# A fused causal convolution and RWKV channel mix: from batch-by-batch chunks to stacked batch pairs and a fixed program order

## The chip, the cores and the metric

One core of a Trainium2 chip runs the whole program. The metric is the device time of one execution in microseconds (us). The core has five engines that run side by side and wait for each other through semaphores: TensorE (PE in the profile; PEld is its weight load), VectorE (DVE), ScalarE (ACT), GpSimd (POOL) and SyncE (SP), whose queue issues DMAs. Each works through its own queue in order.

## The reference

x has 8 batches of 4160 tokens with 192 channels, float32. A causal convolution with 7 taps comes first; its weights are the softmax of an 8 x 7 table, one row for each head of 24 channels. The result goes through a channel mix:

```python
# softmax over the 7 taps, then for every batch, token s, head h
y[s, h] = sum_k w[h, k] * y_in[s + k - 6, h]      # zeros before the first token
x_prev = y shifted down by one token, first row zero
xk = mu_k * y + (1 - mu_k) * x_prev
xr = mu_r * y + (1 - mu_r) * x_prev
k  = maximum(xk @ w_k, 0)          # 192 -> 1024
v  = (k * k) @ w_v                 # 1024 -> 192
r  = sigmoid(xr @ w_r)             # 192 -> 192
out = r * v                        # float32
```

## The kernel before

Batches are processed one after the other, each in 33 blocks of 128 tokens and 9 chunks of 512 tokens (the last of 64). The kernel is written with a planner that orders the instructions of each engine itself; the program's text only gives dependencies and priorities.

Setup (lines 52 to 160): softmax of the taps; its 56 numbers go to DRAM and back so that every partition has them (`w_scr`, `wbc`). From 13 shifted masks, VectorE builds for each head two 128 x 128 banded matrices, `lm` for the block itself (L112, L116) and `lc` for the corner that reaches into the block before (L126, L130). Weights are loaded and cast to bf16 by ScalarE.

For each batch:

- `emit_xload`: for each block of 128 tokens, one DMA of 96 KB brings x (`x_f`, three buffers), and GpSimd casts it to bf16 and sorts it by head (`xb`, L177). The next batch's loads are spread over the chunks of the batch at hand.
- Convolution: for each head two matmuls over up to 21 blocks at once add up in `psum_c` (L196, L203); ScalarE (L211) and VectorE (L216) take turns in copying the result to `y_all`.
- `emit_tr`: each block is transposed in two halves of 96 channels (L225), and copied to `yT` by VectorE (L234) or ScalarE (L238). Channels now lie on partitions, 96 of the 128, twice.
- `emit_mix`: GpSimd forms `diff_t`, the difference of neighbouring tokens (L255); VectorE makes xk and xr from it, two instructions each (L262, L270).
- `emit_kstage`: for each of 8 tiles of d_ff two matmuls of 512 columns into `psum_k` (L289), a relu by ScalarE to `k_sb` (L298), and for each pair of tiles a square by VectorE to `k2_all` (L302; the profile calls it `k_all`).
- `emit_rv`: for each 128 tokens two matmuls for r (L322) and a sigmoid (L329), eight matmuls for v (L338), for each pair a product on VectorE (L349), and one output DMA for each 128 tokens.

In PSUM, `psC` and `psA` (for k) have two buffers each, as have `psB_tr` and `psB_vr`; r and v share the last.

Of the kernel before, what the change touches and what calls it, by code (L numbers as in the profile page):

```python
# [7 lines left out]
FP32 = mybir.dt.float32  # L9
# [6 lines left out]
def kernel(  # L16
# [18 lines left out]
    HC = D // 2  # L35

    NBLK = (S + P - 1) // P
    LAST_ROWS = S - (NBLK - 1) * P
    NB_GRP = 21
    CHUNK = 512  # L40
    NF = DF // P

    const = ctx.enter_context(tc.tile_pool(name="const", bufs=1))
    wpool = ctx.enter_context(tc.tile_pool(name="wts", bufs=1))
    perb = ctx.enter_context(tc.tile_pool(name="perb", bufs=2))
    small = ctx.enter_context(tc.tile_pool(name="small", bufs=3))
    stream = ctx.enter_context(tc.tile_pool(name="stream", bufs=3))
    psA = ctx.enter_context(tc.tile_pool(name="psA", bufs=2, space=bass.MemoryType.PSUM))
    psB = ctx.enter_context(tc.tile_pool(name="psB", bufs=2, space=bass.MemoryType.PSUM))
    dram = ctx.enter_context(tc.tile_pool(name="dram", bufs=1, space=bass.MemoryType.DRAM))  # L50

    w_raw = const.tile([H, K], FP32)
    nc.sync.dma_start(out=w_raw, in_=weight)
# [10 lines left out]
    w_soft = const.tile([H, K], FP32)  # L64
    nc.vector.tensor_scalar(
        out=w_soft, in0=w_exp, scalar1=w_rcp, scalar2=None, op0=ALU.mult
    )
    w_scr = dram.tile([H, K], FP32)
    nc.sync.dma_start(out=w_scr, in_=w_soft)
    wbc = const.tile([P, H, K], FP32)  # L70
    wbc_src = bass.AP(
        tensor=w_scr.tensor,
        offset=w_scr.offset,
        ap=[[0, P], w_scr.ap[-2], w_scr.ap[-1]],
    )
    nc.sync.dma_start(out=wbc, in_=wbc_src)

    ones_t = const.tile([P, P], BF16)
    nc.vector.memset(ones_t, 1.0)
    mmask = []  # L80
    for dlt in range(K):
        m = const.tile([P, P], BF16, tag=f"mmask{dlt}")
        nc.gpsimd.affine_select(
            out=m,
            in_=ones_t,
            pattern=[[1, P]],
            compare_op=ALU.is_equal,
            fill=0.0,
            base=-dlt,
            channel_multiplier=-1,  # L90
        )
        mmask.append(m)
    cmask = {}
    for dlt in range(1, K):
        m = const.tile([P, P], BF16, tag=f"cmask{dlt}")
        nc.gpsimd.affine_select(
            out=m,
            in_=ones_t,
            pattern=[[1, P]],
            compare_op=ALU.is_equal,  # L100
            fill=0.0,
            base=P - dlt,
            channel_multiplier=-1,
        )
        cmask[dlt] = m
    ident = mmask[0]

    Lmain = []
    Lcorner = []
    for h in range(H):  # L110
        lm = const.tile([P, P], BF16, tag=f"lm{h}")
        nc.vector.tensor_scalar(  # L112
            out=lm, in0=mmask[0], scalar1=wbc[:, h, K - 1 : K], scalar2=None, op0=ALU.mult
        )
        for dlt in range(1, K):
            nc.vector.scalar_tensor_tensor(  # L116
                out=lm,
                in0=mmask[dlt],
                scalar=wbc[:, h, K - 1 - dlt : K - dlt],
                in1=lm,  # L120
                op0=ALU.mult,
                op1=ALU.add,
            )
        Lmain.append(lm)
        lc = const.tile([P, P], BF16, tag=f"lc{h}")
        nc.vector.tensor_scalar(  # L126
            out=lc, in0=cmask[1], scalar1=wbc[:, h, K - 2 : K - 1], scalar2=None, op0=ALU.mult
        )
# [12 lines left out]
    wk_sb = wpool.tile([HC, 2, DF], BF16)
    for cc in range(2):
        nc.sync.dma_start(out=wk_f32[:, cc, :], in_=moe_w_k[cc * HC : (cc + 1) * HC, :])
    nc.scalar.copy(out=wk_sb, in_=wk_f32)
    wr_f32 = wpool.tile([HC, 2, D], FP32, tag="wr_f32")
    wr_sb = wpool.tile([HC, 2, D], BF16)
    for cc in range(2):
        nc.sync.dma_start(out=wr_f32[:, cc, :], in_=moe_w_r[cc * HC : (cc + 1) * HC, :])
    nc.scalar.copy(out=wr_sb, in_=wr_f32)
    wv_f32 = wpool.tile([P, NF, D], FP32, tag="wv_f32")  # L150
    wv_sb = wpool.tile([P, NF, D], BF16)
    for f in range(NF):
        nc.sync.dma_start(out=wv_f32[:, f, :], in_=moe_w_v[f * P : (f + 1) * P, :])
    nc.scalar.copy(out=wv_sb, in_=wv_f32)
    mu_f32 = wpool.tile([HC, 2, 2], FP32, tag="mu_f32")
    for cc in range(2):
        nc.sync.dma_start(out=mu_f32[:, 0, cc : cc + 1], in_=moe_mu_k[cc * HC : (cc + 1) * HC])
        nc.sync.dma_start(out=mu_f32[:, 1, cc : cc + 1], in_=moe_mu_r[cc * HC : (cc + 1) * HC])
    mu_bf = wpool.tile([HC, 2, 2], BF16, tag="mu_bf")
    nc.scalar.copy(out=mu_bf, in_=mu_f32)  # L160


    x_bufs = {}

    def emit_xload(bb, jlist):
        if bb not in x_bufs:
            xb = perb.tile([P, H, NBLK + 1, G], BF16, tag="x_bf")
            nc.vector.memset(xb[:, :, 0, :], 0.0)
            x_bufs[bb] = xb
        xb = x_bufs[bb]  # L170
        for j in jlist:
            rows = P if j < NBLK - 1 else LAST_ROWS
            x_f32 = stream.tile([P, D], FP32, tag="x_f32")
            nc.sync.dma_start(
                out=x_f32[:rows, :], in_=x[bb, j * P : j * P + rows, :]
            )
            nc.gpsimd.tensor_copy(  # L177
                out=xb[:rows, :, j + 1, :],
                in_=x_f32[:rows, :].rearrange("p (h g) -> p h g", h=H),
            )  # L180
            if rows < P:
                nc.vector.memset(xb[rows:, :, j + 1, :], 0.0)

    emit_xload(0, range(NBLK))

    for b in range(B):
        x_bf = x_bufs.pop(b)
        yT = perb.tile([HC, 2, 1 + NBLK * P], BF16, tag="yT")
        nc.vector.memset(yT[:, :, 0:1], 0.0)

        y_all = perb.tile([P, NBLK, H, G], BF16, tag="y_all")
        for g0 in range(0, NBLK, NB_GRP):
            nb = min(NB_GRP, NBLK - g0)
            for h in range(H):
                psum_c = psA.tile([P, NB_GRP * G], FP32, tag="psC")
                nc.tensor.matmul(  # L196
                    out=psum_c[:, : nb * G],
                    lhsT=Lmain[h],
                    rhs=x_bf[:, h, g0 + 1 : g0 + 1 + nb, :],
                    start=True,  # L200
                    stop=False,
                )
                nc.tensor.matmul(  # L203
                    out=psum_c[:, : nb * G],
                    lhsT=Lcorner[h],
                    rhs=x_bf[:, h, g0 : g0 + nb, :],
                    start=False,
                    stop=True,
                )
                if h % 2 == 0:  # L210
                    nc.scalar.copy(  # L211
                        out=y_all[:, g0 : g0 + nb, h, :],
                        in_=psum_c[:, : nb * G].rearrange("p (n g) -> p n g", g=G),
                    )
                else:
                    nc.vector.tensor_copy(  # L216
                        out=y_all[:, g0 : g0 + nb, h, :],
                        in_=psum_c[:, : nb * G].rearrange("p (n g) -> p n g", g=G),
                    )

        def emit_tr(jjlist, dve_evac):
            for jj in jjlist:
                psum_tr = psB.tile([P, 2, P], BF16, tag="psB_tr")
                for cc in range(2):
                    nc.tensor.transpose(  # L225
                        out=psum_tr[:HC, cc, :],
                        in_=y_all[:, jj, :, :].rearrange("p h g -> p (h g)")[
                            :, cc * HC : (cc + 1) * HC
                        ],
                        identity=ident,  # L230
                    )
                t0 = jj * P
                if dve_evac:
                    nc.vector.tensor_copy(  # L234
                        out=yT[:, :, 1 + t0 : 1 + t0 + P], in_=psum_tr[:HC, :, :]
                    )
                else:
                    nc.scalar.copy(  # L238
                        out=yT[:, :, 1 + t0 : 1 + t0 + P], in_=psum_tr[:HC, :, :]
                    )  # L240
# [176 lines left out]
```

## Time and profile before

| | |
|---|---|
| three runs | 726.43, 729.37, 730.36 us; median 729.37 |
| span of the profiled execution | 723.8 us; its own whole time is not listed beside it |
| busy: TensorE, VectorE, ScalarE, GpSimd | 605.2, 592.5, 405.3, 296.2 us |
| TensorE matmuls / VectorE instructions | 4576 / 1109 |
| mean granted TensorE clock | 0.960 |
| DMA | 53.72 MB, mean 74 GB/s |

A group row of the profile reads: line, engine, operation, output<-inputs, shapes, count | busy us, mean ns of one | idle time of the engine just before these instructions and what ended it. A timeline row reads: start us, duration us, engine, line, operation, count of the merged instructions, and in brackets the idle time ahead and what ended it. Matmuls overlap in TensorE's pipe, so the mean duration of one is longer than the time that it adds.

### The profile page before, as it was taken

To read this page: it belongs to the slowest core of one execution; us is meant where nothing else is said; L and a number is where in the kernel's file an instruction comes from. 1 tells how busy PE (TensorE), PEld (TensorE's weight loads), DVE (VectorE), ACT (ScalarE), POOL (GpSimd) and SP (SyncE) were. 2 spreads that over 40 slices of the span, in tenths; PEclk is the share of its full clock that TensorE was granted. 3 is DMA by queue.
4 is the path that set the end of the run, shared out by engine and by line. 5 is a ranking of instruction groups with operands and counts; after the bars stand their busy time and mean duration, and the time that the engine had idled before them with its cause. 6 is when DMAs were issued, how large, how long until landed. Compare 5 with 4: busy or idle time off the path is not lost.

```text
span 723.8 us, 13091 instructions
## 1 busy us (share of the span) xinstructions
PE 605.2 (84%) x4576; PEld 396.8 (55%) x4576; DVE 592.5 (82%) x1109; ACT 405.3 (56%) x975; POOL 296.2 (41%) x353
## 2 busy tenths in 40 slices
PE   0268889798898898988898888988898988989977
PEld 0034557555574565645575555745566565645655
DVE  5969997698967999599977789689985889768994
ACT  3027556474566555655565654565565655746554
POOL 3546674476206751176305752067312123022330
PEclk9999989999999999999999998999999899978999
DMA  5413435234112321234112331124111011200112
GB/s 140 121 47 93 119 105 148 72 104 118 37 58 81 102 85 51 64 88 127 50 56 69 110 102 45 56 80 116 58 55 48 1 47 43 67 25 23 45 45 68
DMA packets 77297, 53.72 MB, mean 74 GB/s; under 512 B 9264, under 2 KB 77040, under 8 KB 77232
## 3 DMA queue, kind: packets, MB, share of 16 engines
q1 hardware_dynamic: 77232, 52.90, 24.8%
q8 instruction: 35, 0.57, 0.4%
q14 instruction: 30, 0.25, 0.1%
HBM read 27.31 MB, written 25.56 MB: 73 GB/s over the span
## 4 chain that ended last, share of the span: by engine, by line
PE 52%; DVE 34%; POOL 6%; issue 4%; ACT 3%; DMA 2%; DVEq 0%; POOLq 0%; SPq 0%; ACTq 0%
PE psum_k L289 22%; PE psum_v L338 17%; DVE k_all L302 10%; DVE xk_t L262 7%; DVE xr_t L270 6%; PE psum_r L322 5%; POOL diff_t L255 5%; DVE o_sb L349 4%; PE psum_tr L225 2%; PE psum_c L196 2%; DVE lm L116 2%; PE psum_c L203 2%; DVE yT L234 2%; DVE lc L130 2%; ACT k_sb L298 1%
## 5 line engine op out<-in xcount | busy, mean ns | idle before, releaser
L298 ACT ACTIVATE k_sb<-psum_k 128x512 bf16<-128x512 f32 (+1 forms) x576 | 298.0, 560 | 215.4 <-PE psum_k L289 173.6
L289 PE MATMUL psum_k<-xk_t,wk_sb 96*128 96x512 bf16 (+1 forms) x1152 | 316.2, 377 | 21.4 <-DVE xk_t L262 17.7
L255 POOL TENSOR_TENSOR diff_t<-yT 96x1024 bf16<-96x1024 bf16 (+1 forms) x72 | 143.6, 2000 | 322.2 <-ACT yT L238 173.2
L302 DVE TENSOR_TENSOR k_all<-k_sb 128x1024 bf16<-128x1024 bf16 (+1 forms) x288 | 206.5, 739 | 39.0 <-ACT k_sb L298 38.2
L338 PE MATMUL psum_v<-wv_sb,k_all 128*128 128x192 bf16 (+1 forms) x2112 | 197.5, 247 | 2.0 <-ACT r_all L329 1.8
L338 PEld LDWEIGHTS <-k_all 128*128 128x128 bf16 (+1 forms) x2112 | 178.4, 99 | 25.3 <-issue 5.1
L177 POOL CAST xb<-x_f 128x192 bf16<-128x192 f32 (+1 forms) x264 | 151.1, 588 | 79.2 <-DMA x_f<-in_x_dram 77.7
L289 PEld LDWEIGHTS <-wk_sb 96*128 96x128 bf16 x1152 | 108.8, 101 | 113.0 <-issue 68.5
L262 DVE SCALAR_TENSOR_TENSOR xk_t<-diff_t,mu_bf,yT 96x512 bf16<-96x512 bf16 x144 | 120.5, 839 | 32.1 <-POOL diff_t L255 32.1
L270 DVE SCALAR_TENSOR_TENSOR xr_t<-diff_t,mu_bf,yT 96x512 bf16<-96x512 bf16 x144 | 120.9, 841 | 0.0
L322 PE MATMUL psum_r<-wr_sb,xr_t 96*128 96x192 bf16 x528 | 89.6, 258 | 32.1 <-DVE o_sb L349 23.5
L329 ACT ACTIVATE r_all<-psum_r 128x192 bf16<-128x192 f32 (+1 forms) x264 | 83.3, 338 | 37.8 <-PE psum_r L322 37.5
L322 PEld LDWEIGHTS <-xr_t 96*128 96x128 bf16 x528 | 49.6, 102 | 79.5 <-issue 38.5
L349 DVE TENSOR_TENSOR o_sb<-psum_v,r_all 128x384 f32<-128x384 f32 x128 | 68.7, 548 | 23.3 <-PE psum_v L338 23.1
L225 PE MATMUL psum_tr<-m,y_all 128*96 128x128 bf16 x528 | 68.7, 227 | 21.8 <-DVE yT L234 19.6
L225 PEld LDWEIGHTS <-y_all 128*96 128x96 bf16 x528 | 57.6, 128 | 50.8 <-issue 26.3
L196 PE MATMUL psum_c<-xb,lm 128*128 128x288 bf16 (+1 forms) x128 | 45.0, 356 | 38.0 <-POOL xb L177 30.2
L211 ACT CAST y_all<-psum_c 128x504 bf16<-128x504 f32 (+1 forms) x64 | 31.5, 492 | 50.7 <-PE psum_c L203 49.5
L234 DVE COPY yT<-psum_tr 96x256 bf16<-96x256 bf16 x200 | 49.9, 278 | 3.6 <-PE psum_tr L225 3.1
L216 DVE CAST y_all<-psum_c 128x504 bf16<-128x504 f32 (+1 forms) x64 | 36.1, 565 | 17.4 <-PE psum_c L203 17.3
L203 PE MATMUL psum_c<-xb,lc 128*128 128x288 bf16 (+1 forms) x128 | 45.3, 358 | 0.0
L203 PEld LDWEIGHTS <-lc 128*128 128x128 bf16 x128 | 13.1, 102 | 31.7 <-issue 28.4
(28 smaller groups left out, 88.0 us busy)
## 6 DMA issues: line engine op xcount, KB each, us to landing
x_f<-in_x_dram SPq DMA_DIRECT2D x256, 96.0 KB, 1.9
out_dram<-o_sb SPq DMA_DIRECT2D x256, 96.0 KB, 1.7
wk_f<-in_moe_w_k_dram SPq DMA_DIRECT2D x2, 384.0 KB, 4.0
wv_f<-in_moe_w_v_dram SPq DMA_DIRECT2D x8, 96.0 KB, 2.5
x_f<-in_x_dram SPq DMA_DIRECT2D x8, 48.0 KB, 2.0
out_dram<-o_sb SPq DMA_DIRECT2D x8, 48.0 KB, 1.9
wr_f<-in_moe_w_r_dram SPq DMA_DIRECT2D x2, 72.0 KB, 4.4
mu_f<-in_moe_mu_k_dram SPq DMA_DIRECT2D x2, 0.4 KB, 2.1
```

The lines of the kernel that those rows point to most:

```text
L177: nc.gpsimd.tensor_copy(out=xb[:rows, :, j + 1, :], in_=x_f32[:rows, :].rearrange("p (h g) -> p h g", h=H),)
L225: nc.tensor.transpose(out=psum_tr[:HC, cc, :], in_=y_all[:, jj, :, :].rearrange("p h g -> p (h g)")[:, cc * HC : (cc + 1) * HC], identity= ...
L255: nc.gpsimd.tensor_tensor(out=diff_t[:, :, :L], in0=yT[:, :, 1 + t0 : 1 + t0 + L], in1=yT[:, :, t0 : t0 + L], op=ALU.subtract,)
L262: nc.vector.scalar_tensor_tensor(out=xk_t[:, cc, :L], in0=diff_t[:, cc, :L], scalar=mu_bf[:, 0, cc : cc + 1], in1=yT[:, cc, t0 : t0 + L], ...
L270: nc.vector.scalar_tensor_tensor(out=xr_t[:, cc, :L], in0=diff_t[:, cc, :L], scalar=mu_bf[:, 1, cc : cc + 1], in1=yT[:, cc, t0 : t0 + L], ...
L289: nc.tensor.matmul(out=psum_k[:, :L], lhsT=wk_sb[:, cc, f * P : (f + 1) * P], rhs=xk_t[:, cc, :L], start=(cc == 0), stop=(cc == 1),)
L298: nc.scalar.activation(out=k_sb[:, f % 2, :L], in_=psum_k[:, :L], func=AF.Relu)
L302: nc.vector.tensor_tensor(out=k2_all[:, f - 1 : f + 1, :L], in0=k_sb[:, :, :L], in1=k_sb[:, :, :L], op=ALU.mult,)
L322: nc.tensor.matmul(out=psum_r[:rows, 0, :], lhsT=xr_t[:, cc, m * P : m * P + rows], rhs=wr_sb[:, cc, :], start=(cc == 0), stop=(cc == 1),)
L329: nc.scalar.activation(out=r_all[:rows, m, :], in_=psum_r[:rows, 0, :], func=AF.Sigmoid)
L338: nc.tensor.matmul(out=psum_v[:rows, m % 2, :], lhsT=k2_all[:, f, m * P : m * P + rows], rhs=wv_sb[:, f, :], start=(f == 0), stop=(f == NF ...
L349: nc.vector.tensor_tensor(out=o_sb[:, :npair, :], in0=psum_v[:, :npair, :], in1=r_all[:, m0 : m0 + npair, :], op=ALU.mult,)
```

## The change

The kernel is rewritten, with the same arithmetic:

- Two batches go together, as four pairs. Channels 0 to 127 of the one, those of the other, and the last 64 channels of both stacked on 128 partitions make three slices, so that `yT`, `diff`, `xk` and `xr` have 128 full partitions and three slices for two batches, instead of 96 partitions and two slices for one. For the third slice the weights are held twice, padded with zeros above and below (`wk[:, 1]`, `wk[:, 2]`). The last 64 tokens of both batches make a tail step of its own.
- Convolution blocks have 116 tokens. Their six earlier tokens (the halo) are loaded with them, so one matmul per head does the convolution, over nine blocks of two batches (432 columns). The banded matrix comes from DRAM by an access pattern over a padded copy of the taps, in place of the masks.
- x comes in loads of nine blocks (`load_x`) with one cast each on GpSimd (`cast_x`). Weights are cast by VectorE; their DMAs are issued by ScalarE. The output of 256 tokens leaves in one DMA.
- Convolution copies are all on ScalarE, transpose copies all on VectorE.
- The order on every engine is the program's (`manual_schedule`): slot n does the k matmuls of one d_ff tile for a step of 512 tokens of two batches, the relu of 1024 columns, and the square of the tile before; and tables say which other steps go into which slot. r runs 8 slots behind k, v 10.
- PSUM: two buffers of two banks for k, two for v, and two (`psM`, tag "m") that convolutions, transposes and r share.

The core of the diff (removed lines are those of the listing above):

```diff
+    def load_x(p, g, s):
+        xf = xfp.tile([P, GB, D], FP32, tag="xf")          # 3 buffers
...
+        nc.sync.dma_start(out=xf[:, lo:hi, :], in_=src)     # blocks of 116 with 6 tokens of halo
...
+    w_scr = dram.tile([H, P, W], BF16)
+    nc.sync.dma_start(out=w_scr, in_=w_row.unsqueeze(1).to_broadcast([H, P, W]))
+    toe = const.tile([P, H, BLK], BF16)
+    nc.sync.dma_start(out=toe, in_=bass.AP(tensor=w_scr.tensor, offset=w_scr.offset + K - 1,
+            ap=[[W - 1, P], [P * W, H], [1, BLK]]))
...
+    def cast_x(p, g, s):
+        nc.gpsimd.tensor_copy(
+            out=xbs[p, g][:, :, :, s, :], in_=xf.rearrange("p n (h g) -> p h n g", h=H))
+    def conv_mm(p, g, h):
+        ps = psM.tile([P, GB, 2, G], FP32, tag="m", name="ps_c")
+        nc.tensor.matmul(out=ps[:BLK].rearrange("p n s g -> p (n s g)"), lhsT=toe[:, h, :],
+            rhs=xb[:, h, :, :, :].rearrange("p n s g -> p (n s g)"), start=True, stop=True)
+    def conv_out(p, g, h):
+        if c0 < P:
+            nc.scalar.copy(out=yh[:, :, :, c0 : c0 + n], in_=ps[:BLK, :, :, 0:n])
+        if c1 > P:
+            nc.scalar.copy(out=yl[:, :, :, c1 - P - n : c1 - P], in_=ps[:BLK, :, :, G - n : G])
+    def tr_mm(p, g, j):
+        ps = psM.tile([P, 3, 2, BLK], BF16, tag="m", name="ps_t")
+        for i in range(min(2, GB - 2 * j)):
+            for c in range(3):
+                nc.tensor.transpose(out=ps[:, c, i, :],
+                    in_=ys[p, g][:BLK, 2 * j + i, c * P : (c + 1) * P], identity=ident[:BLK, :BLK])
+    def tr_out(p, g, j):
+        nc.vector.tensor_copy(out=yTs[p][:, :, c0 : c0 + n * BLK]..., in_=ps[:, :, :n, :])
+    def diff(p, s):
+        nc.gpsimd.tensor_tensor(out=d[:, :, :L], in0=yT[:, :, c0 : c0 + L],
+            in1=yT[:, :, c0 - 1 : c0 - 1 + L], op=ALU.subtract)
+    def mix(p, s, i, part):          # part 0: slices 0 and 1 in one instruction; part 1: slice 2
+            nc.vector.scalar_tensor_tensor(out=o, in0=d[r0:r1, sl, :L],
+                scalar=mu[r0:r1, i, part : part + 1], in1=yT[r0:r1, sl, c0 : c0 + L],
+                op0=ALU.mult, op1=ALU.add)
+    def k_mm(n):
+            ps = psK.tile([P, 2, STEP], FP32, tag="k", name="ps_k")
+            for i in range(2):
+                nc.tensor.matmul(out=ps[:, i, :], lhsT=wk[:, 0, fs], rhs=xk[:, i, :], start=True, stop=False)
+            for i in range(2):
+                nc.tensor.matmul(out=ps[:, i, :], lhsT=wk[:, 1 + i, fs], rhs=xk[:, 2, :], start=False, stop=True)
...
+    def k_relu(n):
+        k_sb = four.tile([P, 2 * STEP], BF16, tag="k_sb", name="k_sb")
+        nc.scalar.activation(out=k_sb, in_=ps.rearrange("p a b -> p (a b)"), func=AF.Relu)
+    def k_square(n):
+            if f == 0:
+                k2s[p, s] = three.tile([P, NF, 2 * STEP], BF16, tag="k2", name="k2")
...
+        nc.vector.tensor_tensor(out=o, in0=k_sb, in1=k_sb, op=ALU.mult)
+    def r_mm(m):                     # two matmuls per 128 tokens, a psM buffer for each two m
+            r_ps[q] = psM.tile([P, 2, D], FP32, tag="m", name="ps_r")
...
+    def r_sig(m):
+        nc.scalar.activation(out=r_sb[:, :n, :], in_=ps[:, :n, :], func=AF.Sigmoid)
+    def v_mm(m):                     # eight matmuls per 128 tokens, a psV buffer for each two m
...
+    def v_out(m):
+        nc.vector.tensor_tensor(
+            out=o_sb[:, :n, :], in0=v_ps.pop(m)[:, :n, :], in1=r_sbs.pop(m)[:, :n, :], op=ALU.mult)
+            nc.sync.dma_start(
+                out=out[b, t0 : t0 + 2 * P, :].rearrange("(m p) d -> p m d", p=P), in_=o_sb)
+    for p in range(NPAIR):
+        for g in range(NG):
+            n0 = p * SPP + 2 * g * NF
+            for s in range(2):
+                if (p, g) != (0, 0):
+                    at(early, n0 - 44 + 6 * s, load_x, p, g, s)
+                at(pool, n0 - 34 + 6 * s, cast_x, p, g, s)
+            for h in range(H):
+                at(pe, n0 - 22 + h, conv_mm, p, g, h)
+                at(act, n0 - 21 + h, conv_out, p, g, h)
+            for j in range((GB + 1) // 2):
+                at(pe, n0 - 13 + j, tr_mm, p, g, j)
+                at(dve, n0 - 12 + j, tr_out, p, g, j)
+        for s in range(NSTEP + 1):
+            n0 = p * SPP + s * NF
+            at(pool, n0 - 7, diff, p, s)
+            for i in range(2):
+                for part in range(2):
+                    at(dve, n0 - 5 + 2 * i + part, mix, p, s, i, part)
+    for m in range(NSLOT):
+        p, s, t = where(m)
+        at(pe, m + LAG_R, r_mm, m)           # LAG_R = 8
+        last = t % 2 == 1 or s == NSTEP
+        if last:
+            q = m - t % 2
+            at(act, m + LAG_R + 1, r_sig, q)
+            at(dve, m + LAG_V + 1, v_out, q)  # LAG_V = 10
+        at(pe, m + LAG_V, v_mm, m)
+    with tc.manual_schedule():
+        for n in range(-60, NSLOT + LAG_V + 3):
+            run(early, n)
+            run(pool, n)
+            if 0 <= n < NSLOT:
+                k_mm(n)
+            run(act, n)
+            run(pe, n)
+            if 0 <= n < NSLOT:
+                k_relu(n)
+            run(dve, n)
+            if 1 <= n <= NSLOT:
+                k_square(n - 1)
```

567 lines of the change are left out of this document (270 added, 297 removed).

## The prediction

> **What bounds the kernel now.** I read the page first, then the chain, the groups kept apart by shape, the waits, and the timeline. The page's engine line:
>
> ```profile
> span 723.8 us, 13091 instructions
> PE 605.2 (84%) x4576; PEld 396.8 (55%) x4576; DVE 592.5 (82%) x1109; ACT 405.3 (56%) x975; POOL 296.2 (41%) x353
> PEclk9999989999999999999999998999999899978999
> q1 hardware_dynamic: 77232, 52.90, 24.8%
> ```
>
> TensorE is busy 84%, at a granted clock of nine tenths and more in most slices, but its matmuls overlap in the pipe, so I count what a matmul adds when it follows another. The chain says who ends last:
>
> ```profile
> PE 52%; DVE 34%; POOL 6%; issue 4%; ACT 3%; DMA 2%; DVEq 0%; POOLq 0%; SPq 0%; ACTq 0%
> ```
>
> No engine carries it: it changes hands between TensorE and VectorE. The groups by shape:
>
> ```profile
> L289 PE MATMUL psum_k<-xk_t,wk_sb 96*128 96x512 bf16 x1024 | 306.2, 401 | 21.4 <-DVE xk_t L262 17.7 <-ACT k_sb L298 3.0
> L298 ACT ACTIVATE k_sb<-psum_k 128x512 bf16<-128x512 f32 x512 | 286.9, 600 | 200.2 <-PE psum_k L289 158.4 <-DVE k_all L302 30.6 <-PE psum_c L203 2.5
> L302 DVE TENSOR_TENSOR k_all<-k_sb 128x1024 bf16<-128x1024 bf16 x256 | 199.3, 804 | 32.4 <-ACT k_sb L298 31.7
> L338 PE MATMUL psum_v<-wv_sb,k_all 128*128 128x192 bf16 x2048 | 190.7, 247 | 1.6 <-ACT r_all L329 1.4
> L255 POOL TENSOR_TENSOR diff_t<-yT 96x1024 bf16<-96x1024 bf16 x64 | 137.1, 2145 | 322.2 <-ACT yT L238 173.2 <-DVE yT L234 138.5 <-issue 9.7
> L262 DVE SCALAR_TENSOR_TENSOR xk_t<-diff_t,mu_bf,yT 96x512 bf16<-96x512 bf16 x128 | 116.3, 909 | 32.1 <-POOL diff_t L255 32.1
> L329 ACT ACTIVATE r_all<-psum_r 128x192 bf16<-128x192 f32 x256 | 80.7, 338 | 17.7 <-PE psum_r L322 17.3
> L349 DVE TENSOR_TENSOR o_sb<-psum_v,r_all 128x384 f32<-128x384 f32 x128 | 68.7, 548 | 23.3 <-PE psum_v L338 23.1
> L225 PE MATMUL psum_tr<-m,y_all 128*96 128x128 bf16 x528 | 68.7, 227 | 21.8 <-DVE yT L234 19.6 <-ACT yT L238 1.3 <-DVE y_all L216 0.9
> L211 ACT CAST y_all<-psum_c 128x504 bf16<-128x504 f32 x32 | 18.7, 583 | 37.3 <-PE psum_c L203 36.2
> L298 ACT ACTIVATE k_sb<-psum_k 128x64 bf16<-128x64 f32 x64 | 11.2, 234 | 15.2 <-PE psum_k L289 15.2
> L255 POOL TENSOR_TENSOR diff_t<-yT 96x128 bf16<-96x128 bf16 x8 | 6.7, 840 | 0.0
> L262 DVE SCALAR_TENSOR_TENSOR xk_t<-diff_t,mu_bf,yT 96x64 bf16<-96x64 bf16 x16 | 4.2, 278 | 0.0
> L83 POOL TENSOR_SCALAR_AFFINE_SELECT m<-ones_t 128x128 bf16<-128x128 bf16 x7 | 1.8, 295 | 0.6 <-DVE ones_t L79 0.6
> ```
>
> For the cost in a queue I take runs of one kind from the timeline (start, duration, engine, line, count); n of them in t, each d long, follow each other by (t-d)/(n-1):
>
> ```profile
> 716.15 2.80 PE L338 MATMUL psum_v<-wv_sb,k_all 128*128 128x192 bf16 x32
> 697.89 1.03 PE L289 MATMUL psum_k<-xk_t,wk_sb 96*128 96x512 bf16 x4
> 698.52 1.08 ACT L298 ACTIVATE k_sb<-psum_k 128x512 bf16<-128x512 f32 x2 [2.33 <-PE psum_k L289]
> 672.44 0.39 PE L225 MATMUL psum_tr<-m,y_all 128*96 128x128 bf16 x4
> 412.49 1.08 ACT L298 ACTIVATE k_sb<-psum_k 128x512 bf16<-128x512 f32 x2
> 702.43 0.56 ACT L329 ACTIVATE r_all<-psum_r 128x192 bf16<-128x192 f32 x2
> 444.60 1.88 DVE L302 TENSOR_TENSOR k_all<-k_sb 128x1024 bf16<-128x1024 bf16 x3
> 686.41 0.73 DVE L262 SCALAR_TENSOR_TENSOR xk_t<-diff_t,mu_bf,yT 96x512 bf16<-96x512 bf16 x1
> 687.07 0.74 DVE L270 SCALAR_TENSOR_TENSOR xr_t<-diff_t,mu_bf,yT 96x512 bf16<-96x512 bf16 x1
> 409.09 1.01 DVE L349 TENSOR_TENSOR o_sb<-psum_v,r_all 128x384 f32<-128x384 f32 x2
> 400.98 0.47 DVE L234 COPY yT<-psum_tr 96x256 bf16<-96x256 bf16 x2
> ```
>
> So in us: v matmul .082, k matmul .215, transpose .054, relu of 512 .48, sigmoid .22, square .60 (d is .68 undisturbed), mix of 512 .66, output product .46, transpose copy .19; and a handover of .2, from the stream of two k matmuls (697.89 + .43) to their relu (698.52). TensorE's own work before: 1024 x .215, 2112+528 of 192 columns x .082, 528 x .054, convolutions 128 at .212 and 128 at .121 (.215 by columns), tails 4: 511 us. The other 213 us of the span TensorE waits or runs slowed, some 45 of them before the first k matmul at 50.89 (row below).
>
> **The change, part by part.** One slot is now a d_ff tile of a step of two batches; 4 x 65 = 260 slots.
>
> TensorE. k: four matmuls of 512 columns per slot for two batches, 1024 x .215 = 220, unchanged: the 64 rows left over of each batch's 192 take a full matmul of their own, with weights padded by zeros. Tails 64 x .055 = 4. v 2080 x .082 = 171, r 520 x .082 = 43. Convolution: one matmul of 432 columns per head instead of two, 128 x .181 = 23 (was 43). Transposes 432 of 116 columns x .051 = 22; its weight loads have 128 columns, which this trace bears out only at .082, so 22 to 35; I take 22, the nearer instruction. Sum 483, 28 less than before. So most of the gain must come from waits.
>
> By the Trainium skill, page TensorE: Matmul & The Clock Gate, section Back-to-back issue gap, a stream of loads and matmuls sustains about 131 ns at 512 columns, which would make k 134 us and the sum 86 us less. The trace disagrees, 215 ns at L289, so no chance hangs on it.
>
> ScalarE. Relu of 1024: .48 + 512 x .82 ns ((600-234)/448) = .90; conv copies 432 wide, about .40, nine per group; sigmoid over a pair .38. In 16 slots 14.4+3.3+3.0 = 20.7 us: slack.
>
> VectorE. Squares 16 x .60; mixes of 128 partitions, two slices in one instruction: .66 + 512 x 1.03 ns ((740-278)/448) = 1.19 and .66, four of each in 16 slots = 7.4 (was 16 x .66 = 10.6); transpose copies of 696 elements between .42 and .65 (half or whole of 1.03 ns an element); the copy of 256 in .19 is faster than the whole, so .43, 2.0 in all; output products 8 x .47. Conv copies leave for ScalarE. Sum 22.8 us in 16 slots, against TensorE's 16 x 1.68 + 8 x .181 + 27 x .051 = 29.7.
>
> GpSimd, and what it takes from VectorE. Diff grows to 1536 elements: 1.89 + 512 x 1.17 ns ((1890-840)/896) = 2.49 us. Nine casts become one of 1728: from .35 + 1536 x .78 ns ((345-295)/64 against L83) = 1.55 us, to 9 x .35 = 3.1; I take 1.55, since the count of elements and not of instructions stays. These hold VectorE:
>
> ```profile
> 672.33 1.89 POOL L255 TENSOR_TENSOR diff_t<-yT 96x1024 bf16<-96x1024 bf16 x1 [6.07 <-DVE yT L234]
> 672.48 2.28 DVE L302 TENSOR_TENSOR k_all<-k_sb 128x1024 bf16<-128x1024 bf16 x1
> 417.12 0.35 POOL L177 CAST xb<-x_f 128x192 bf16<-128x192 f32 x1 [0.42 <-DMA x_f<-in_x_dram]
> 405.47 0.82 DVE L270 SCALAR_TENSOR_TENSOR xr_t<-diff_t,mu_bf,yT 96x512 bf16<-96x512 bf16 x1
> ```
>
> A square begun .15 after a diff ends .54 after it: it stood until .14 before the diff's end. A mix beside casts loses only .08. So in 16 slots two diffs hold 2 x 2.35 and two casts, I take their growing part, 2 x 1.2; of that 75% hits (squares and mixes are 17.0 of 22.8): 5.3. VectorE then needs 28.1, between 22.8 (nothing hits) and 34.0 (all of 2 x 2.49 + 2 x 3.1): just under TensorE.
>
> By the Trainium skill, page SBUF — State Buffer, section Who interferes with whom, a VectorE instruction with two SBUF inputs and a GpSimd one that reads SBUF exclude each other for the whole instruction, which speaks against fewer, longer GpSimd instructions. The trace agrees for the diff (2.28 against .68), less so for the cast. By the rule the 16 slots cost VectorE 22.8 + 8.1 = 30.9.
>
> Waits in the fixed order. The pool psM has two buffers for convolutions, transposes and r. A convolution two on waits for the sigmoid that stands on ScalarE behind relu and conv copy: .86 (k) + .2 + .90 + .40 + .50 = 2.86 against 1.86 + .86 = 2.72 when TensorE asks, with half a handover more about .25, in four of eight slots: 1.0. Transposes in slots 3 to 7 of 16 want their copy back from VectorE while the four mixes, and a cast, stand in slots 3 to 6: VectorE needs 3.7 + 5 x .60 + 4 x .43 + 1.2 = 9.6 and 1.2 of lock there against TensorE's 5 x 1.68 + 27 x .051 = 9.8, so it is late by 1.0, with the handovers about 1.5. Behind that wait stand r and v on TensorE. Together 2.5 us in 16 slots; x 16.25 = 41 us. Bounds: .5 and 6 (both locks at 3.1 and 2.5 inside the transposes), 8 to 98. Buffers elsewhere (k_sb four, psV two pairs, v two slots behind the last square) take a lateness of 3.7 us, so they cost 0 unless VectorE falls behind for good.
>
> Start and end.
>
> ```profile
> 4.44 0.28 SPq L69 DMA_DIRECT2D w_scr<-w_soft  x1
> 7.08 0.33 SPq L76 DMA_DIRECT2D wbc<-w_scr  x1
> 10.10 0.25 DVE L112 TENSOR_SCALAR lm<-m,wbc 128x128 bf16<-128x128 bf16 x1 [5.68 <-DMA wbc<-w_scr]
> 50.89 0.58 PE L289 MATMUL psum_k<-xk_t,wk_sb 96*128 96x512 bf16 x1 [1.11 <-DVE xk_t L262]
> 719.64 0.82 PE L338 MATMUL psum_v<-wv_sb,k_all 128*64 128x192 bf16 x8 [0.41 <-ACT r_all L329]
> ```
>
> The 104 VectorE instructions that built the masks (L112 to L130, to 39 us) go; the matrix comes by two DMA hops. Softmax ends at 4.4 as before. The first hop (.50 MB) queues on SP behind 1.77 MB of x, beside 2 MB of weights on ScalarE's queue: at 295 GB/s (52.90 MB in 24.8% of 723.8 us) 9 to 15 us, so the second leaves about 17 and lands about 22 (a hop was 2.6 to 3.0; bounds 12 without queueing, 30). The next x loads stand behind it on SP, land by 26, and are cast before the diff. Eight convolutions at .65 (copy and hops, two buffers), transposes, diff 2.5, mix 1.85: first k matmul at 34.7, between 26 and 45. Weight casts (now VectorE) lie under that. Output DMAs halve in number, off the path. Then 478 us of TensorE (483 less what is done before), 2 for a cold clock (this profile starts with k matmuls .38 to .43 apart), 3.3 from last v to end.
>
> Sum: 34.7 + 478 + 41 + 2 + 3.3 = 559 against the span of 723.8. The median 729.4 lies 5.6 above the span: 565.
>
> **Rivals.**
> A, TensorE alone bounds (stalls .5 in 16 slots): 565 - 33 = 532. For it: slack of two slots nearly everywhere. Against: psM.
> B, VectorE with GpSimd's lock bounds: 34.0 in 16 slots with the 2.5 on top, 16.25 x 36.5 + 40 + 6 = 639; by 30.9 and none on top 548, inside the forecast. For it: the 2.28 row; against: casts lose .08.
> C, waits stay in proportion: before, 213-45 = 168 on 511, or 33%. 478 x 1.33 + 46 (start, end and what lies around the span) = 682. For it: two-buffer PSUM pools as before. Against: then whole chunks waited for a late diff (322.2 us idle ahead of L255 on yT), now made seven slots ahead.
> D, slower: every conv and transpose slot becomes a round trip through psM, because r and v stand behind it. Conv slot .86+.90+.40+.38+.4 = 2.94, transpose slot .86+1.19+.60+.43+.47+.2 = 3.75: mean of 16 (8, 5, 3 at 1.68) 2.96, 260 x 2.96 + 44 = 814. It decides from 2.63 us a slot, .77 of wait in each; I find .16.
> That the order isn't kept: excluded, each engine's queue is the program.
>
> **How the numbers follow.** Forecast (stalls 1 to 4.5 in 16 slots, 540 to 600) .60, A .12, B .14, C .08, D .04, rest .02 (start, on either side). Time 565. Range 528 to 630: A below, the likelier half of B above; C, D and B's end left out, about .18. Measurement tells 0.5%: faster .95, same .01, slower .04.
>
> **What would show it.** First k matmul at 35; k matmuls .215 and v .082 apart; TensorE granted near 1.0; a transpose or convolution matmul waiting on VectorE copies or the sigmoid, some 40 us in all; squares over 2 us beside diffs; a diff of 2.5 and a cast of 1.6. Wrong if a cast is 3 us or holds all of it (B), if the start passes 45, or if k_sb or k2 waits show VectorE behind for good.

## The result, and the profile after

The changed kernel takes 548.86 us (median of four runs, 547.81 to 549.68) against 727.9 us before (median of four, 725.39 to 730.36): a ratio of 0.7546, with a 95% interval of 0.7517 to 0.7575. The profiled execution took 549.68 us with a span of 548.0.

The page of the changed kernel: engines, granted clock, chain, and the groups that answer to those of before.

```profile
span 548.0 us, 10694 instructions
PE 498.3 (91%) x4248; PEld 359.5 (66%) x4248; DVE 488.6 (89%) x643; ACT 377.9 (69%) x539; POOL 172.7 (32%) x88
...
PEclk9999999999999999999999999999999999999999
...
PE 68%; DVE 17%; issue 7%; DMA 6%; POOL 1%; ACT 1%; SPq 0%; DVEq 0%; POOLq 0%
...
L355 DVE TENSOR_TENSOR k<-k_sb 128x1024 bf16<-128x1024 bf16 x256 | 254.5, 1005 | 5.6 <-ACT k_sb L341 5.1
L390 PE MATMUL ps_v<-wv,k 128*128 128x192 bf16 x2048 | 211.2, 246 | 3.8 <-DVE o_sb L402 2.7
...
L310 PE MATMUL ps_k<-xk,wk 128*128 128x512 bf16 x512 | 153.6, 382 | 2.2 <-DVE xk L277 2.2
```

TensorE now carries 68% of the chain (52% before). Its mean granted clock is 0.999 (0.960 before). Both engines are near 90% busy, and yet the k and v matmuls have hardly any idle time ahead of them: 2.2 us (L310; 2.1 for L314) and 3.8, where `psum_k` alone had 21.4.

To see where the 176 us went, I split both spans at TensorE: start of the first matmul, its stream (each matmul counted with the step of its kind, as in the prediction), waits (what lies beyond that step between one start and the next, summed), and the rest behind the last start.

| us | first matmul | stream | waits | rest | span |
|---|---|---|---|---|---|
| before | 29.7 | 514.8 | 175.6 | 3.6 | 723.8 |
| after | 30.4 | 484.3 | 28.9 | 4.2 | 548.0 |

(A delay of less than 8 ns is not counted, so the parts may miss the span by .2.)

So 30 us come from a shorter stream and 147 from what the table calls waits. Not all of that is waiting: some of it is matmuls at half the clock. In the profile before, TensorE was granted .50 in twelve stretches, 58 us in all; here is one of them (length, then busy time and instructions of TensorE, its loads, VectorE, ScalarE, GpSimd; granted clock; DMA share; GB/s):

```profile
99.90:106.70 6.80, 5.83 (x22) 3.05 (x22) 6.21 (x13) 3.21 (x7) 4.80 (x5) 0.50 0.39 115
```

The k matmuls in it stand (1.91 - .63)/3 = .43 us apart, twice their step:

```profile
103.48 1.91 PE L289 MATMUL psum_k<-xk_t,wk_sb 96*128 96x512 bf16 x4
```

In these stretches the matmuls took 26 us more than their steps. The changed kernel has no such stretch until its last microsecond. (Both kernels also run their first matmuls at twice the step, for some 6.5 us more.) So about 26 of the 147 us are the clock's and about 120 are waits. The largest waits of TensorE behind the first matmul, before (total us, times, longest):

```profile
PE psum_r L322 <- DVE o_sb L349: 23.5, 26, 2.0
PE psum_tr L225 <- DVE yT L234: 19.6, 18, 2.6
PE psum_k L289 <- DVE xk_t L262: 17.7, 20, 2.6
```

All three are for VectorE. What TensorE waits for now stands in the changed kernel's waits:

```profile
POOL d L255 <- DVE yT L239: 239.0, 16, 23.7
...
PE ps_c L198 <- DMA toe<-w_scr: 30.4, 1, 30.4
...
ACT k_sb L341 <- DVE k L355: 9.2, 12, 1.0
...
PE ps_r L371 <- DVE yT L239: 3.2, 4, 0.8
PE ps_v L390 <- DVE o_sb L402: 2.7, 5, 1.8
PE ps_t L229 <- DVE yT L239: 2.3, 4, 0.8
```

The one large wait is for the banded matrix at the start. GpSimd's 239 us ahead of `d` are nobody's loss. Two stretches of the changed kernel's timeline show the start and the holds:

```profile
7.95 0.84 SPq L116 DMA_DIRECT2D w_scr<-w_row  x1
...
22.68 0.37 SPq L118 DMA_DIRECT2D toe<-w_scr  x1
...
30.40 0.97 PE L198 MATMUL ps_c<-xb,toe 128*116 128x432 bf16 x2 [30.40 <-DMA toe<-w_scr]
...
41.45 5.76 DVE L277 SCALAR_TENSOR_TENSOR xk<-d,mu,yT 128x1024 bf16<-128x1024 bf16 x2 [2.42 <-POOL d L255]
...
42.94 3.72 POOL L255 TENSOR_TENSOR d<-yT 128x1536 bf16<-128x1536 bf16 x1
...
44.11 1.01 PE L310 MATMUL ps_k<-xk,wk 128*128 128x512 bf16 x2 [2.19 <-DVE xk L277]
...
307.88 2.75 POOL L255 TENSOR_TENSOR d<-yT 128x1536 bf16<-128x1536 bf16 x1 [13.79 <-DVE yT L239]
...
308.12 3.06 DVE L355 TENSOR_TENSOR k<-k_sb 128x1024 bf16<-128x1024 bf16 x1
...
310.57 2.08 POOL L186 CAST xb<-xf 128x1728 bf16<-128x1728 f32 x1
...
311.35 1.85 DVE L355 TENSOR_TENSOR k<-k_sb 128x1024 bf16<-128x1024 bf16 x1
311.48 0.24 PE L371 MATMUL ps_r<-wr,xr 128*128 128x192 bf16 x1 [0.85 <-DVE yT L239]
```

A square of .68 takes 3.06 beside a diff, and 1.85 beside a cast; the first ends .55 after the diff, so it stood until about the end of that. TensorE goes on beside both, but for .85 us ahead of the matmul at 311.48, whose buffer waits for a transpose copy that stood behind the first of these squares.

### The profile page after: what moved, and what is told of

The parts are those of the page before. It is cut to its first block, busy times and chain, and to the rows that moved or that the text cites. A ratio compares the mean times of both kernels' runs of the same rounds, so it can differ in the third digit from the quotient of the medians.

```text
span 548.0 us, 10694 instructions
## 1 busy us (share of the span) xinstructions
PE 498.3 (91%) x4248; PEld 359.5 (66%) x4248; DVE 488.6 (89%) x643; ACT 377.9 (69%) x539; POOL 172.7 (32%) x88
## 4 chain that ended last, share of the span: by engine, by line
PE 68%; DVE 17%; issue 7%; DMA 6%; POOL 1%; ACT 1%; SPq 0%; DVEq 0%; POOLq 0%
PE ps_v L390 25%; PE ps_k L314 15%; PE ps_k L310 15%; DVE k L355 7%; DVE xk L277 4%; PE ps_r L371 3%; PE ps_r L372 3%; PE ps_c L198 3%; DMA xf<-in_x_dram 3%; PE ps_t L229 3%; DMA w_scr<-w_row 3%; DVE o_sb L402 2%; DVE xr L277 2%; DVE yT L239 2%; ACT k_sb L341 1%
## 5 line engine op out<-in xcount | busy, mean ns | idle before, releaser
L341 ACT ACTIVATE k_sb<-ps_k 128x1024 bf16<-128x1024 f32 x260 | 265.9, 1023 | 120.7 <-PE ps_k L314 108.7
L355 DVE TENSOR_TENSOR k<-k_sb 128x1024 bf16<-128x1024 bf16 x256 | 254.5, 1005 | 5.6 <-ACT k_sb L341 5.1
L390 PE MATMUL ps_v<-wv,k 128*128 128x192 bf16 x2048 | 211.2, 246 | 3.8 <-DVE o_sb L402 2.7
L390 PEld LDWEIGHTS <-k 128*128 128x128 bf16 x2048 | 173.5, 98 | 39.9 <-issue 5.8
L255 POOL TENSOR_TENSOR d<-yT 128x1536 bf16<-128x1536 bf16 (+1 forms) x36 | 102.2, 2841 | 275.6 <-DVE yT L239 239.0
L310 PE MATMUL ps_k<-xk,wk 128*128 128x512 bf16 x512 | 153.6, 382 | 2.2 <-DVE xk L277 2.2
L314 PE MATMUL ps_k<-xk,wk 128*128 128x512 bf16 x512 | 153.6, 382 | 2.1 <-DVE xk L277 2.1
L314 PEld LDWEIGHTS <-wk 128*128 128x128 bf16 x512 | 50.4, 98 | 63.7 <-issue 4.0
L402 DVE TENSOR_TENSOR o_sb<-ps_v,r_sb 128x384 f32<-128x384 f32 x132 | 71.8, 544 | 12.2 <-PE ps_v L390 10.3
L277 DVE SCALAR_TENSOR_TENSOR xr<-d,mu,yT 128x1024 bf16<-128x1024 bf16 x64 | 77.0, 1205 | 0.9
L198 PE MATMUL ps_c<-xb,toe 128*116 128x432 bf16 x128 | 46.6, 370 | 31.8 <-DMA toe<-w_scr 30.4
L371 PE MATMUL ps_r<-wr,xr 128*128 128x192 bf16 x256 | 63.0, 246 | 3.3 <-DVE yT L239 3.2
L372 PE MATMUL ps_r<-wr,xr 128*128 128x192 bf16 x256 | 63.0, 246 | 0.0
L310 PEld LDWEIGHTS <-wk 128*128 128x128 bf16 x512 | 46.4, 98 | 4.3 <-issue 4.2
L198 PEld LDWEIGHTS <-toe 128*116 128x116 bf16 x128 | 17.6, 139 | 48.1 <-DMA toe<-w_scr 30.4
```

What stands on the lines that cost most here:

```text
L198: nc.tensor.matmul(out=ps[:BLK].rearrange("p n s g -> p (n s g)"), lhsT=toe[:, h, :], rhs=xb[:, h, :, :, :].rearrange("p n s g -> p (n s g)"),
L255: nc.gpsimd.tensor_tensor(out=d[:, :, :L], in0=yT[:, :, c0 : c0 + L], in1=yT[:, :, c0 - 1 : c0 - 1 + L], op=ALU.subtract,)
L277: nc.vector.scalar_tensor_tensor(out=o, in0=d[r0:r1, sl, :L], scalar=mu[r0:r1, i, part : part + 1], in1=yT[r0:r1, sl, c0 : c0 + L], op0=AL ...
L310: nc.tensor.matmul(out=ps[:, i, :], lhsT=wk[:, 0, fs], rhs=xk[:, i, :], start=True, stop=False)
L314: nc.tensor.matmul(out=ps[:, i, :], lhsT=wk[:, 1 + i, fs], rhs=xk[:, 2, :], start=False, stop=True)
L341: nc.scalar.activation(out=k_sb, in_=ps.rearrange("p a b -> p (a b)"), func=AF.Relu)
```

## The experiments

Theory: TensorE's stream sets the time after the start. VectorE, with what GpSimd holds of it, needs almost as long, but falls behind only for moments (an instruction is called held when it lasts longer beside GpSimd's than alone), which slack of about two slots in the fixed order takes up. Rivals: the gain is TensorE's smaller stream alone; the order is worth little; GpSimd's holds are free, or hit TensorE directly; the start depends on the DMA load and not on its own chain.

**The order left to the planner.**

```diff
-    with tc.manual_schedule():
+    if True:
```

> The same program with the order left to the planner instead of the fixed order; all instructions and buffers are the same. Theory (the fixed order removes TensorE's waits: before, TensorE lost about 159 us after its first k matmul beside its own stream of columns, now 16 us): the waits come back in part, 575 to 640 us. Rival (the stacking and the larger instructions alone bring the gain, the order nothing): within 1% of 549 us.

Measured: 582.06 us, ratio 0.8027 [0.7992, 0.8061]. 33 us are the order's. Waits rise from 28.9 to 63.1 at the same stream. The planned kernel's waits:

```profile
PE ps_v L390 <- DVE o_sb L402: 27.5, 15, 2.4
```

This was 2.7 in the fixed order: v finds both of its PSUM pairs still unread, because VectorE's output products stand behind other work; ahead of 11 of these 15 waits that is a mix of 3.2 to 3.8 us beside a diff (1.28 undisturbed). The other 146 of the 179 us come with the rest of the change; no run separates its parts (the stacking, the larger instructions, the convolution with a halo).

**The diffs on GpSimd left out.** The mixes read `yT`, shifted by one, in place of d.

```diff
-        nc.gpsimd.tensor_tensor(out=d[:, :, :L], in0=yT[...], in1=yT[...], op=ALU.subtract)
...
-                in0=d[r0:r1, sl, :L],
+                in0=yT[r0:r1, sl, c0 + 1 : c0 + 1 + L],
```

> GpSimd's differences of neighbouring tokens are left out; the mixes read the transposed tile itself in their place, so xk and xr are not those of the reference. This takes away 36 GpSimd instructions of about 2.8 us and the time for which they hold VectorE, and leaves every other engine its instructions. Theory (TensorE's stream bounds, VectorE's held time is hidden): 537 to 545 us, by the 2.75 us of the first difference ahead of the first k matmul and a part of the 16 us of later waits. Rival (the held VectorE sets the pace): 525 us or less.

Measured: 535.70 us, ratio 0.7393 [0.7349, 0.7437], a little below what I expected. Its groups:

```profile
L349 DVE TENSOR_TENSOR k<-k_sb 128x1024 bf16<-128x1024 bf16 x256 | 186.0, 729 | 30.8 <-ACT k_sb L335 30.3
```

The squares lose 68.5 us (254.5 to 186.0), and the kernel only 13, of which some 3 are an earlier first matmul (27.5): most of the held time was taken up.

**The diffs doubled.**

```diff
+        for _ in range(2):
             nc.gpsimd.tensor_tensor(out=d[:, :, :L], ...)
```

> Each GpSimd difference is done twice in a row; the result is the same. Theory (VectorE with what GpSimd takes from it is just under TensorE, 29.6 against 29.7 us in 16 slots, so it becomes the bound at once): 32 x 2.7 = 86 us more of held time, less some slack: 605 to 640 us. Rival (VectorE has slack of several us in 16 slots and TensorE alone bounds): below 560 us.

Measured: 647.79 us, ratio 0.8932 [0.8892, 0.8972], 99 us more, above what I expected. Its waits:

```profile
PE ps_v L391 <- DVE o_sb L403: 68.3, 21, 6.9
```

One diff more per step doesn't fit into the slack that is left; the wait is the planned kernel's, with a longest of 6.9. (By the split above, TensorE's delays are 129.4 us in this run, some 30 of them in stretches at half the clock; whether these add to the time beside VectorE's, no run separates.) Taking one diff away gives 13 us and adding one costs 99, so the kernel stands just ahead of a knee.

**Less work for TensorE.** The k matmuls of the third slice are left out: 512 x .215 = 110 us of a stream of 484.

```diff
-            for i in range(2):
-                nc.tensor.matmul(
-                    out=ps[:, i, :], lhsT=wk[:, 1 + i, fs], rhs=xk[:, 2, :], start=False, stop=True)
```

> The 512 k matmuls of the third slice (the last 64 channels of each batch) are left out, 110 us of TensorE's stream; k is then computed from 128 of the 192 channels. All other instructions stay. Theory (VectorE and TensorE are near co-bounds): VectorE keeps the pace, 16.25 x 29.6 + 53 = 534, so 522 to 545 us. Rival (TensorE alone bounds): 439 to 460 us.

Measured: 533.85 us, ratio 0.7359 [0.7331, 0.7387]: 15 us for 110. Its page:

```profile
PE 413.4 (78%) x3736; PEld 313.3 (59%) x3736; DVE 487.4 (92%) x643; ACT 368.3 (69%) x539; POOL 171.1 (32%) x88
...
DVE 59%; issue 20%; PE 12%; DMA 5%; ACT 2%; POOL 1%; SPq 0%; DVEq 0%; POOLq 0%
```

The chain goes over to VectorE, whose 487 us are those of the changed kernel. VectorE was only some 15 us from being the bound.

**The two hops of the matrix issued by ScalarE,** with mu and the weights behind the first x loads on SP.

```diff
-    nc.sync.dma_start(out=w_scr, ...)      # and toe
+    nc.scalar.dma_start(out=w_scr, ...)
...
-        nc.scalar.dma_start(out=mu[...], ...)   # and the weights
+        nc.sync.dma_start(out=mu[...], ...)
```

> Only queues are changed: the padded taps and the banded matrix (L116, L118) are issued by ScalarE instead of standing behind the x loads on SP, and mu and the weights are issued by SP behind the first two x loads. Theory (the start, first k matmul at 44.1 us, is set by the banded matrix that lands at 30.4 us behind x): it lands at 20 us or earlier, the first k matmul stands at 36 us or earlier, 535 to 542 us in all. Rival (the DMA engines are full at the start, so the order of the queues doesn't matter): 546 to 551 us.

Measured: 555.21 us, ratio 0.7631 [0.7603, 0.7659]: slower than the changed kernel, a miss. Its timeline:

```profile
5.13 1.27 ACTq L116 DMA_DIRECT2D w_scr<-w_row  x1
...
27.06 0.38 ACTq L118 DMA_DIRECT2D toe<-w_scr  x1
35.79 0.97 PE L198 MATMUL ps_c<-xb,toe 128*116 128x432 bf16 x2 [35.79 <-DMA toe<-w_scr]
```

The first hop was issued 2.8 us earlier and the second 4.4 later. The chain of this run has the first hop from issue to landing (start, length):

```profile
5.13 14.15 DMA w_scr<-w_row
```

A window shows the DMA engines with hardly anything beside it (columns as in the window row above):

```profile
12.00:18.00 6.00, 0.00 (x0) 0.00 (x0) 0.00 (x0) 0.00 (x0) 0.22 (x1) 1.00 0.34 42
```

So its place in the queue, to which I had put it down, was not what made the first hop long: almost alone it moved at 42 GB/s and took 14.15 us. But it had landed at 19.3, 3.4 us before the second hop leaves in the changed kernel. That the second left only at 27.06 has another reason, which I had overlooked: in the trace it waits for a semaphore that it shares with a load of w_r, issued on SP at 21.47, and the last update from that load comes at 27.04. So 7.8 us of this start are lost to the weights that the edit put ahead of it, and the miss does not show that an earlier first hop is worth nothing.

**The difference on VectorE.**

```diff
-        nc.gpsimd.tensor_tensor(out=d[:, :, :L], ...)
+        nc.vector.tensor_tensor(out=d[:, :, :L], ...)
```

> The differences move from GpSimd to VectorE, at the same place of the program order. An instruction of 1536 elements costs VectorE between .9 us (at the rate of a square, .60 for 1024) and 1.7 us (at the rate of a mix, 1.03 ns an element), and takes away 2.1 us or more of held time each. Theory (TensorE's stream bounds, with 16 us of later waits that come from held VectorE): 536 to 545 us. Rival (VectorE, nearly full, pays for the added instruction): 550 us or more.

Measured: 538.25 us, ratio 0.7397 [0.7364, 0.7430], 10.6 us faster than the changed kernel. Its groups by shape:

```profile
L355 DVE TENSOR_TENSOR k<-k_sb 128x1024 bf16<-128x1024 bf16 x256 | 184.8, 724 | 15.2 <-ACT k_sb L341 13.8
...
L255 DVE TENSOR_TENSOR d<-yT 128x1536 bf16<-128x1536 bf16 x32 | 31.3, 979 | 0.0
```

VectorE takes on 31.3 us of diffs and gets 69.7 back on its squares. Offloading to GpSimd had cost the engine that it was meant to relieve.

**Both of these.** The edits of the last two runs together.

> Both edits together: the banded matrix early and the differences on VectorE. Theory: the two gains add, since one lies ahead of the first k matmul and the other behind it: 522 to 534 us. Rival (they overlap): as the better of the two alone.

Measured: 544.43 us, ratio 0.7482 [0.7454, 0.7510]. A miss, with the start's (its second hop waits for the same load): the gain of d on VectorE adds to that loss (555.21 - 10.8).

**The kernel before without its second mixes** (r is computed from `xk_t`): VectorE has 121 us less to do (116.7 + 4.1).

```diff
-                nc.vector.scalar_tensor_tensor(out=xr_t[:, cc, :L], ...)   # L270
...
-            xrs[ci] = xr_t
+            xrs[ci] = xk_t
```

> The kernel before, without the second pair of mixes (L270): r is computed from xk, so the second mix of the reference is left out, and with it 121 us of VectorE's busy time. What held the kernel before? If VectorE's load (592 us) did, 610 to 650 us. If TensorE and VectorE wait for each other in turn (the chain of before has L270 with 6%, 43 us): 670 to 700 us. If the load of VectorE played no part: above 715 us.

Measured: 700.35 us, ratio 0.9626 [0.9575, 0.9678]: -27 for -121. Its page:

```profile
PE 592.6 (84%) x4576; PEld 393.8 (56%) x4576; DVE 490.3 (70%) x965; ACT 398.3 (57%) x975; POOL 292.5 (42%) x353
```

The first row of TensorE in its timeline:

```profile
42.67 0.58 PE L196 MATMUL psum_c<-xb,lm 128*128 128x504 bf16 x1 [42.67 <-POOL xb L177]
```

The planner put the start 13 us later here (29.67 before); between the first and the last matmul 36 us are gone. VectorE at 70% still leaves 140 us of TensorE's delays by the split above (21 of them at half the clock). So VectorE's load alone was not the bound of the kernel before; this fits engines that wait for each other in turn, just outside the 670 to 700 that I had put under it.

**A small scratch row for the matrix.** The first hop writes 8 x 256 values (4 KB) in place of .50 MB; the second reads the matrix's rows from it with a step of +1, and a reversed constant matrix in the transposes undoes the reversed order of the tokens.

```diff
-    w_scr = dram.tile([H, P, W], BF16)
-    nc.sync.dma_start(out=w_scr, in_=w_row.unsqueeze(1).to_broadcast([H, P, W]))
+    w_scr = dram.tile([H, W], BF16)                 # W = 256
+    nc.scalar.dma_start(out=w_scr, in_=w_row)       # taps from column 115 on, not reversed
...
-            ap=[[W - 1, P], [P * W, H], [1, BLK]],
+            ap=[[1, P], [W, H], [1, BLK]],          # toe, issued by ScalarE
...
-        base=0, channel_multiplier=-1,              # ident
+        base=1 - BLK, channel_multiplier=1,
```

> The changed kernel with the banded matrix loaded from a scratch row of 8 x 256 values (4 KB) in place of 8 x 128 x 244 (.50 MB): the rows of the matrix are read with a step of +1 instead of a pitch of 243, which gives them with the tokens of a block in reverse, and the transposes' constant matrix is reversed to undo it. Both hops are issued on ScalarE's queue, behind wk; mu and the weights stay where they are. Theory 1 (the start is set by the matrix, and its landing by the first hop's own transfer from 8 partitions): the first hop lands about 2.6 us after its issue, the matrix between 14 and 22 us (30.4 in the changed kernel), the first k matmul 13.7 us after that at most, at 28 to 36 (44.1): time 535 to 541. Theory 2 (the landing is set by the load on the DMA engines, whoever issues first, as when the queues were changed alone): the matrix lands at 26 or later, time 544 to 552.

Measured: 542.11 us, ratio 0.7464 [0.7441, 0.7487], between the two expectations. Its timeline:

```profile
7.60 0.53 ACTq L116 DMA_DIRECT2D w_scr<-w_row  x1
...
12.87 0.40 ACTq L118 DMA_DIRECT2D toe<-w_scr  x1
...
21.28 0.97 PE L198 MATMUL ps_c<-xb,toe 128*116 128x432 bf16 x2 [21.28 <-DMA toe<-w_scr]
...
27.41 0.96 DVE L170 CAST wv<-stage 128x1536 bf16<-128x1536 f32 x1 [4.24 <-DMA stage<-in_moe_w_v_dram]
...
36.31 1.01 PE L310 MATMUL ps_k<-xk,wk 128*128 128x512 bf16 x2 [2.19 <-DVE xk L277]
```

From issue to issue the hops are now 5.3 us apart (14.7 in the changed kernel). Another queue alone, above, left the first hop at 14.15 us to its landing, so its own transfer was the cause; whether by its bytes, its 1024 rows of 488 bytes or its 8 partitions, no run separates. The second still takes 8.4 us beside x and weights (7.7 before the edit). In the other runs it took 4.8 (the planned kernel) to 8.7, so what else is under way seems to set that half; no run takes it away. And a new wait comes up: VectorE stands for 4.2 us at the cast of `wv`, ahead of the transpose copies. So 9.1 us earlier at the first matmul are 7.8 at the first k.

**The small row and the difference on VectorE together.**

> The same small scratch row and, with it, the difference d computed on VectorE. By theory 1 the two gains add, since one lies before the first k matmul and the other after: the run with d on VectorE had 538.2 and its first k matmul at 42.3, 11.7 us after its first convolution matmul; with the matrix at 14 to 22 us the first k is at 28 to 34 and the time 524 to 530. By theory 2 534 to 540.

Measured: 532.20 us (four runs, 531.83 to 533.06), ratio 0.7327 [0.7304, 0.7350], 2 us above what theory 1 gave. The gains add (548.9 - 6.8 - 10.6 = 531.5). It beats both kernels, the changed one by 3%. The chain on its page:

```profile
PE 83%; DVE 7%; DMA 4%; issue 3%; ACT 1%; ACTq 0%; DVEq 0%
```

Its longest waits of TensorE behind the one for the matrix:

```profile
PE ps_t L229 <- DVE yT L239: 6.8, 7, 1.5
```

From the first start (20.8) to the last (525.6) TensorE waits 20.5 us beside its 484.3 (70 matmuls are missing from this trace, so I took the stream of the changed kernel). What is left to gain is its stream.

**The slack taken away.** Two buffers for `k_sb` in place of four, and v one slot earlier.

```diff
-    LAG_V = NF + 2
+    LAG_V = NF + 1
...
-        k_sb = four.tile([P, 2 * STEP], BF16, tag="k_sb", name="k_sb")
+        k_sb = two.tile([P, 2 * STEP], BF16, tag="k_sb", name="k_sb")
```

> The changed kernel with two buffers for k_sb in place of four and v one slot earlier (one slot behind the last square in place of two); the work is the same. Theory 1 (squares held by GpSimd cost little because slots of slack absorb them): a square held by a diff for 2.5 us now reaches TensorE but for one slot's slack of 1.7 us or less, so each of 32 diffs costs .8 to 2.5 us: 26 to 80 us more, 575 to 630. Theory 2 (the slack is not used, the held time would have been free anyway since VectorE has idle time between instructions): 546 to 553.

Measured: 587.29 us, ratio 0.8076 [0.8048, 0.8105]: 38 us more for the same work. Its waits:

```profile
ACT k_sb L341 <- DVE k L355: 67.7, 61, 3.3
...
PE ps_c L198 <- ACT y L214: 26.0, 35, 2.5
```

Its timeline beside a held square:

```profile
306.74 3.23 DVE L355 TENSOR_TENSOR k<-k_sb 128x1024 bf16<-128x1024 bf16 x1
...
310.07 1.02 ACT L341 ACTIVATE k_sb<-ps_k 128x1024 bf16<-128x1024 f32 x1 [3.30 <-DVE k L355]
...
311.55 0.34 PE L198 MATMUL ps_c<-xb,toe 128*116 128x432 bf16 x1 [2.49 <-ACT y L214]
```

ScalarE's waits for a square go from 9.2 us to 67.7, and TensorE's for a convolution copy from 1.0 to 26.0. A square held for 2.5 us holds the relu behind it, that the convolution copy, and that a convolution matmul: 2.49 us on TensorE. The holds are nearly the same as in the changed kernel (100.3 us against 96.6 after the first k matmul, in what instructions last beyond their undisturbed time); there the buffers swallow them.

## Why the prediction was right, and where its terms were off

565 was forecast with a range of 528 to 630, and 548.86 came. The mechanism held: TensorE's stream bounds, VectorE with its holds comes just under it, and the gain is mostly waits. That the time comes as near as 16 us is in part luck: the terms that were too small miss 13.6 us in all, those that were too large 28.5, and nearly half of that cancels. The terms, against the profiled execution:

| us | predicted | measured |
|---|---|---|
| first k matmul | 34.7 | 44.1 |
| TensorE's stream after it | 478 | 480.5 |
| waits after it | 41 | 16.4 |
| cold clock | 2 | 2.8 |
| end | 3.3 | 4.2 |
| span | 559 | 548.0 |
| around the span | 5.6 | 1.7 |

*The cold clock* shows in the rows around 52 us, where the k matmuls go from .43 apart to .215:

```profile
51.35 1.01 PE L314 MATMUL ps_k<-xk,wk 128*128 128x512 bf16 x2
52.20 0.60 PE L310 MATMUL ps_k<-xk,wk 128*128 128x512 bf16 x2
52.63 0.59 PE L314 MATMUL ps_k<-xk,wk 128*128 128x512 bf16 x2
```

The 5.6 *around the span* set the span of one execution against the median of others. The later runs of the kernel before list both for each execution; there they lie 2.0 to 3.4 us apart.

*TensorE's stream* came out step by step: k .215 apart, v and r .082, convolution .182, transposes .050. For these I had taken the lower end of 22 to 35 us, and it was the right one.

*VectorE* needs 22.7 us undisturbed in 16 slots (22.8 predicted), and 5.9 held (5.3): 96.6 us after the first k, by what each instruction lasts beyond the undisturbed one of its shape; 51 of the 61 held ones are squares. The undisturbed diff was 2.75 (2.49 predicted) and the cast 1.62 (1.55). By the Trainium skill, page SBUF — State Buffer, section Who interferes with whom, the cast too excludes a two-input VectorE instruction. The rows agree more than I had granted: the square at 311.35 waited until about the end of the cast at 312.65. That a cast holds all of an instruction was one of my signs of being wrong, towards B. But 28.6 us in all is less than the 30.9 that I had worked out by that rule, and stays under TensorE's 29.7: the diffs and casts last 155 us after the first k matmul, and held VectorE for 96.6.

*The start* failed in the step that has the first hop (.50 MB) queue on SP behind x: it left at 7.95 and not at 4.4, and the second followed at 22.68 and not at 17. For the late departure the trace shows a semaphore that the hop shares with the first x load and that this load updates last at 7.88. For the rest, the load on the DMA engines, from which I took these times, was not the reason; the small row, and the 14.15 us that the hop took almost alone, show its own transfer in its place. The second then took 7.7 us and not 5. And I had priced the two first mixes at 1.85 undisturbed, and left out that the second diff and a cast stand beside them (5.76 at 41.45): the first k matmul at 44.11 is followed by its third slice only at 47.27.

*The waits* were mis-sized by more than half: 16.4 us for 41. I had a transpose slot late by 1.5 us and a convolution late by 1.0 in every 16 slots. The rows show waits of transposes and r on `yT` of 5.5 us in all (2.3 + 3.2), in four places each: after the start and where the tail step's work falls in. Elsewhere VectorE comes in time, since the holds fall on squares, and these have slack. That the slack does it is shown by the run without it, which brought back the round trip through psM: 26.0 us in 35 waits of up to 2.5.

*The rivals.* A (532, stalls near none) is what the best version is, with its start mended and d on VectorE. B (VectorE bounds) was close: with less work for TensorE the kernel stays at 533.9, and with one diff more per step it takes 647.8 (that B gave 639 for other holds is no check of its terms). C fell. D's mechanism showed in the run without slack, at 38 us and not at 265.

## What to carry to other kernels

Before moving work to GpSimd, price what its instructions hold of VectorE, by the row of a VectorE instruction beside one and alone; 31 us of diffs on VectorE were cheaper than 100 us of them beside it. A hold or a late copy costs nothing as long as the order leaves it a slot of slack, so count the slots before pricing it, and test by taking the slack away. Where a chain of DMA hops sets the start, look at each hop's transfer (its bytes, rows and partitions) and at the semaphores that it shares with other loads, and not only at the queue that it stands in.

## What was not expected of the hardware

The window from 16 to 24 us of the changed kernel (columns as in the window rows above; the last is GB/s):

```profile
16.00:24.00 8.00, 0.00 (x0) 0.00 (x0) 1.90 (x4) 0.00 (x0) 1.18 (x1) 1.00 0.67 143
```

The same window of the kernel with the small scratch row:

```profile
16.00:24.00 8.00, 2.29 (x5) 1.01 (x6) 3.10 (x7) 1.88 (x4) 1.63 (x1) 1.00 1.13 299
```

While a .50 MB transfer out of 8 partitions was under way, all queues together moved 143 GB/s; with a row of 4 KB in its place the loads went at 299 in the same window. The granted clock was 0.999 with TensorE 91% busy in the changed kernel, 0.960 at 84% before, and 0.937 at 82% with the diffs doubled; but 0.983 at 78% without the third slice, so the busy share alone does not set it, and what does stays open. And the difference of 1536 elements took .95 us on VectorE, undisturbed, against 2.75 on GpSimd.
